# Four modulation rows in one dense product, spread by way of HBM; a tail without identity products; a last block in halves

## The chip, the core and the metric

One core of a Trainium2 chip runs the whole kernel. The metric is the device time of one execution in microseconds (us). The engines are TensorE (PE in the profile, with PEld for its weight loads), VectorE (DVE), ScalarE (ACT), GpSimd (POOL) and SyncE (SP), which here does nothing but issue DMA transfers, in order.

## What is computed

An adaLN block: a modulation from `c`, a sliding-window attention, and an MLP over the tokens. S = 2048 tokens, D = 512, 32 heads of 16, a window of 256, F = 1792.

```python
mod = (silu(c) @ w_mod).reshape(1, 6, 1, 512)          # six rows of 512
sa, ca, ga, sb, cb, gb = mod[:, 0], ..., mod[:, 5]
h = layernorm(x) * (1 + ca) + sa
x = x + ga * (attention(h, wqkv, window=256) @ wo)
h = layernorm(x) * (1 + cb) + sb
u = gelu(einsum('bsd,sf->bdf', layernorm(h), w1) + b1)  # contracts the tokens
y = (u @ w2 + b2).transpose(0, 2, 1)
x = x + gb * y
```

The four rows ga, cb, sb and gb multiply or shift along the free dimension, so the kernel keeps each as a tile of 128 equal rows of 512 (`bc_ga`, `bc_cb1`, which holds 1 + cb, `bc_sb`, `bc_gb`).

## The kernel before

The 2048 tokens are 16 blocks of 128 (`tb`), in four groups of four (`tg`). There are five stages.

- Head (to about 15 us): loads, LayerNorm of group 0, the feature-major rows sa and ca (`modFM`), Q, K and V of the first heads. GpSimd builds constants and masks; a memset of `ones` (L196) releases ScalarE's first copies (L406).
- Attention (about 15 to 171 us): 80 units, 20 for each group. A unit (`ul` = 5 * g8 + k, from 0 to 19) covers eight heads g8 and one of five kinds k of score pieces. For each unit TensorE makes scores into PSUM (`pss`, a ring of three tiles), ScalarE takes their exponential in two instructions (`et`, L573), and TensorE multiplies by V into `po` (L584, L600). After kinds 2 and 4 VectorE transposes `po` (`t`, L632); a reciprocal on VectorE (`zr`), a division on GpSimd (`merge`, L644) and a transpose back on VectorE (`OTd`, L652) follow.
- Tail of the attention (about 171 to 180 us): `t_wo` makes the output projection of the last four blocks: four products with `wod`, then a fifth product that adds the residual through the identity, and a copy out of PSUM by ScalarE (L964 to L969). LayerNorms of these blocks run on VectorE (t1, t2, t3), while TensorE goes on with the first six F-chunks of the MLP (`emit_b1_group0_sc`, L942).
- First MLP product (to 217 us, L942 and L1029), then GELU.
- Second MLP product (to the end, L1049): for each group 14 products per block. The last group runs block after block; VectorE finishes a block in two instructions (L1056, L1061) and SP stores it (L1062).

The order of the attention is written out by hand. `plan(tg)` lays dense work on units (`at[ul]`): Q and K groups, V groups, transposes of the next group's LayerNorm (`transpose_group`), the output projection of the group before (`wo_group`, with LayerNorms 2 and 3 behind it, `ln23`), and in group 0 the four `bc_group`s on units 9, 16, 17 and 18. Each group is 16 matmuls on 32-column strips of the array (`dense`, L274) into the only buffer of the pool `ps_dn`; a group's evacuation by VectorE must be over before the next group starts. In each unit TensorE gets, in this order: the scores of the next unit, the AV product of the unit before if it closes a pair, the dense group, else that AV product.

The steps of VectorE and GpSimd that hang on none of this are chains (`add_chain`), put between the evacuations by a planner: `fill(until)` takes the first chain whose step is ready by the plan's `clock` and fits. `clock` adds up assumed costs; a step that goes on on GpSimd returns its cost there (`on_pool`), and the next step of its chain is not placed before that. Both engines then run their lists strictly in order, so a list that is wrong about a cost makes an engine wait at the head of its queue. `fold_wod` (four multiplications of `wod` by `bc_ga` on GpSimd) is such a chain, added at unit 14 of group 0; `wo_group` needs all four.

Loads are paced: `paced` holds a load back until the first exponential of its unit is over. The parts of `w_mod` for the four rows go out at units 2 to 9 of group 0 (two halves a row, in the order ga, cb, sb, gb), `wo` at units 10 and 11, pieces of `w1` from unit 2 of group 1 on. SP also issues small copies `Vc<-VaugT` (L610).

```python
at.get(ul)                      # one dense group a unit, between scores and AV
for ul, (v, dst, add1) in zip((9, 16, 17, 18), BC):
    lay(ul, bc_group(v, dst, add1, ps_dn))
then[14] = [(lambda g=g: fold_wod(g), 0.0) for g in range(ND)]
```

## Time and profile before

| | us |
|---|---|
| median of 3 runs | 270.45 |
| lowest, highest | 268.9, 270.62 |
| the profiled execution's own time | 271.25 |
| its span, first to last instruction | 269.5 |
| PE busy, DVE busy, ACT busy, POOL busy | 244.3, 165.9, 166.0, 129.0 |
| granted TensorE clock, mean | 0.993 |

A line of the timeline has the start in us, the busy time in us, engine, line of the kernel, operation, output and inputs, shape and count, and in square brackets the idle time before it and what ended that. In a table by windows the columns are window, and for each engine its busy time with the count of instructions, then the granted clock, the DMA engines' busy share and GB/s.

### The profile page before, as it was taken

The page shows a single profiled execution, that of the slowest core. Times are in us where ns is not written, and L with a number is a line of the kernel's source. Part 1 is how long each engine was busy: PE and PEld are TensorE (multiplying, and loading weights), DVE is VectorE, ACT ScalarE, POOL GpSimd, SP SyncE. Part 2 cuts the span into 40 slices and gives each one's busy share as a digit, 9 for nine tenths or more (in the row PEclk, how much of TensorE's full clock was granted, in tenths as well). Part 3 has the DMA queues.
Part 4 walks back from the last instruction along what each step waited for, and adds up shares of the span by engine and source line. Part 5 has one row for each costly group of instructions (what it writes and reads, how often), then busy time and mean ns, then how long its engine had stood idle before and what let it go on. Part 6 is the DMA issues. An engine that isn't in the chain of part 4 may idle for free.

```text
span 269.5 us, 11147 instructions
## 1 busy us (share of the span) xinstructions
PE 244.3 (91%) x4971; PEld 129.4 (48%) x4971; DVE 165.9 (62%) x345; ACT 166.0 (62%) x193; POOL 129.0 (48%) x220
## 2 busy tenths in 40 slices
PE   6978769999899889878889989999999999999993
PEld 2534444455565455545555546544444444444441
DVE  6568965886689787699687886689111000523443
ACT  7777874899999999989999999330091110000000
POOL 6104953876376899888977699864100000000000
PEclk9999997999999999999999999999999999999999
DMA  6918880015654443000122000899900000202021
GB/s 188 356 46 218 243 260 21 5 32 151 182 171 121 130 127 92 6 2 5 31 56 70 5 5 2 272 412 416 394 11 2 0 0 0 80 0 78 27 93 39
DMA packets 25221, 29.31 MB, mean 109 GB/s; under 512 B 3156, under 2 KB 22612, under 8 KB 25172
## 3 DMA queue, kind: packets, MB, share of 16 engines
q1 hardware_dynamic: 25172, 28.59, 33.2%
q8 instruction: 39, 0.64, 1.0%
q14 instruction: 10, 0.08, 0.1%
HBM read 22.03 MB, written 2.10 MB: 90 GB/s over the span
## 4 chain that ended last, share of the span: by engine, by line
PE 66%; DVE 16%; POOL 6%; ACT 5%; issue 3%; DMA 3%; SPq 0%; POOLq 0%; DVEq 0%; ACTq 0%
PE py L1049 18%; PE dn L274 17%; PE pu L942 8%; PE pu L1029 8%; PE pss L523 4%; PE po L584 3%; DVE VaugT L290 3%; PE po L600 3%; DMA wmod<-in_w_mod_dram 3%; DVE t L632 2%; ACT et L573 2%; DVE qs L312 2%; PE pss L530 1%; POOL QT L316 1%; DVE h1T L264 1%
## 5 line engine op out<-in xcount | busy, mean ns | idle before, releaser
L573 ACT ACTIVATE et<-pss 128x1024 bf16<-128x1024 f32 (+1 forms) x160 | 143.7, 992 | 14.0 <-PE pss L530 12.1
L1049 PE MATMUL py<-guT,w2r 128*128 128x512 bf16 x224 | 48.5, 380 | 0.0
L1056 DVE SCALAR_TENSOR_TENSOR o<-py,bFM,bc_gb 128x512 bf16<-128x512 f32 x16 | 11.4, 747 | 44.7 <-PE py L1049 44.7
L274 PE MATMUL dn<-h1T,wqkv 128*32 128x512 bf16 x512 | 34.3, 388 | 3.7 <-DVE qs L312 1.5
L1049 PEld LDWEIGHTS <-w2r 128*128 128x128 bf16 x224 | 21.9, 98 | 26.4
L523 PE MATMUL pss<-QT,KT 32*128 32x64 bf16 (+2 forms) x704 | 28.2, 239 | 5.5 <-ACT et L573 3.0
L632 DVE STREAM_TRANSPOSE t<-po 128x512 f32<-128x512 f32 x32 | 22.6, 706 | 7.8 <-PE po L600 7.7
L214 POOL TENSOR_TENSOR ln_rstd<-ln_ve,mhalf 128x1 f32<-128x1 f32 (+1 forms) x40 | 24.0, 601 | 3.3
L523 PEld LDWEIGHTS <-KT 32*128 32x128 bf16 x704 | 15.0, 93 | 21.2 <-issue 11.8
L584 PE MATMUL po<-et,VaugT 128*32 128x64 bf16 (+2 forms) x704 | 25.2, 242 | 0.0
L210 POOL TENSOR_SCALAR ln_ve<-ln_mv 128x1 f32<-128x1 f32 (+1 forms) x40 | 9.4, 235 | 33.0 <-DVE ln_mv L232 18.4
L584 PEld LDWEIGHTS <-VaugT 128*32 128x32 bf16 x704 | 17.5, 97 | 10.8 <-issue 1.6
L274 PEld LDWEIGHTS <-wqkv 128*32 128x32 bf16 x512 | 13.0, 96 | 13.5 <-issue 6.2
L644 POOL TENSOR_TENSOR merge<-t,zr 128x512 bf16<-128x512 f32 x16 | 16.9, 1056 | 4.8 <-DVE zr L643 4.8
L530 PE MATMUL pss<-mask_q,mask_k 32*128 32x256 bf16 (+1 forms) x256 | 19.1, 264 | 0.0
L274 PE MATMUL dn<-wqkv,h1T 128*32 128x512 bf16 x240 | 15.8, 382 | 1.8 <-DVE VaugT L290 0.8
L676 POOL TENSOR_TENSOR h<-h,bc_cb 128x512 bf16<-128x512 bf16 x12 | 13.9, 1155 | 5.1 <-DVE h L672 5.1
L274 PE MATMUL dn<-wod,OTd 128*32 128x512 bf16 x192 | 12.6, 381 | 3.1 <-DVE KT L309 1.3
L677 POOL TENSOR_TENSOR h<-h,bc_sb 128x512 bf16<-128x512 bf16 x12 | 13.9, 1154 | 0.9
L316 POOL TENSOR_SCALAR QT<-qs,mask_even 128x512 bf16<-128x512 bf16 x14 | 9.7, 692 | 8.8 <-DVE qs L312 8.7
L942 PE MATMUL pu<-hb,w1a 128*128 128x512 bf16 x60 | 13.5, 380 | 0.0
L600 PE MATMUL po<-et,Vc 128*32 128x64 bf16 x960 | 13.1, 195 | 0.0
(113 smaller groups left out, 360.6 us busy)
## 6 DMA issues: line engine op xcount, KB each, us to landing
w2r<-in_B_w_dram SPq DMA_DIRECT2D x14, 512.0 KB, 9.9
w1a<-in_B_w_dram SPq DMA_DIRECT2D x20, 224.0 KB, 3.1
w1b<-in_B_w_dram SPq DMA_DIRECT2D x6, 448.0 KB, 6.9
Vc<-VaugT SPq DMA_DIRECT2D x32, 64.0 KB, 3.0
wmod<-in_w_mod_dram SPq DMA_DIRECT2D x8, 256.0 KB, 5.1
out_dram<-otile SPq DMA_DIRECT2D x16, 128.0 KB, 1.8
x<-in_A_x_dram SPq DMA_DIRECT2D x6, 256.0 KB, 5.1
Vc<-VaugT SPq DMA_DIRECT2D x12, 128.0 KB, 3.3
```

The source lines that it names most:

```text
L214: nc.gpsimd.tensor_tensor(out=r[:], in0=ve[:], in1=mhalf[:, 0:n], op=ALU.pow)
L274: nc.tensor.matmul(out[cols, :], lhsT=lhsT[:, cols], rhs=rhs, start=start, stop=stop, tile_position=(0, 32 * j), skip_group_check=True,)
L523: nc.tensor.matmul(pss[j // 2][:, j % 2, c0 : c0 + nq], lhsT=keys(kb, g8)[rows[j], k0 : k0 + P], rhs=QT[tg][g8][rows[j], par, q0 : q0 + nq ...
L530: nc.tensor.matmul(pss[j // 2][:, j % 2, :].rearrange("p (a r) -> p a r", a=2)[:, 0:n, :] .rearrange("p a (b q) -> p a b q", q=64)[:, :, 0 ...
L573: act = nc.scalar.activation(out=et[:, :, 0:n], in_=state.pop((u, a))[:, :, 0:n], func=ACT.Exp, scale=SCORE_SCALE,)
L584: nc.tensor.matmul(state["po"][32 * j : 32 * j + 32, q0 : q0 + nq], lhsT=VaugT[kb // 4][:, kb % 4, 8 * g8 + 2 * j + par, :], rhs=state["e" ...
L600: nc.tensor.matmul(state["po"][32 * j : 32 * j + 32, q0 : q0 + 64], lhsT=Vc[half][:, b, 8 * g8 + 2 * j + par, :], rhs=state["e", tg, g8, 2 ...
L632: nc.vector.transpose(out=state["t2"][:, par, :], in_=state["po"][:])
L644: nc.gpsimd.tensor_tensor(out=m[:].rearrange("p (b a d) -> p a b d", a=2, d=DH), in0=t2v[:, :, :, 0:DH], in1=zr[:].to_broadcast([P, 2, 16, ...
L942: nc.tensor.matmul(pu[:, i, :], lhsT=w1_of(sc, fc), rhs=hb[sc][:], start=(sc == 0), stop=(sc == NT - 1),)
L1029: nc.tensor.matmul(pu[:, i, :], lhsT=w1_of(sc, fc), rhs=hb[sc][:], start=(sc == s0), stop=(sc == NT - 1),)
L1049: nc.tensor.matmul(pys[tl][:], lhsT=w2r[:, fc, tb * P : (tb + 1) * P], rhs=guT[fc][:], start=(fc == 0), stop=(fc == NF - 1),)
```

## The change

Six edits.

1. `sT_rep` keeps 32 instead of 128 copies of silu(c). One group `bc_group(ps_dn)` on unit 13 makes all four rows at once: strip j of 32 partitions holds row j. One VectorE instruction evacuates it to `mod_rows` and adds `mod_add` (a column that is 1.0 on the second strip). SP writes `mod_rows` to a buffer in HBM and reads it back with four loads of 32 partitions x 4 rows into one tile `bc`. Two memsets on GpSimd make `mod_add`.
2. In group 0, V of the next group moves from units 13 and 19 to units 16 and 18, and the folding of `wod` is added at unit 18 instead of 14.
3. The planner's assumed GpSimd costs change: p2 2.31 to 2.4, p3 1.8 to 2.0, LayerNorm 1's apply 0.95 to 1.13, the allowance after a GpSimd step 0.1 to 0.3.
4. The planner's assumed TensorE times for a unit of kind 2 change: 0.5 to 0.3 and 0.58 to 0.42.
5. `t_wo` drops the product with the identity and ScalarE's copy; VectorE adds the residual while it evacuates.
6. The last block of the last product is made and finished in two halves of 256 columns.

Because the planner reads the changed costs, the lists of VectorE and GpSimd differ in places that the diff does not show. In groups 1 to 3 the scaling `h` (L672) mostly comes later on VectorE, behind the residual additions of `wo_group`; at the end of group 3 two LayerNorm statistics stand between `zr` and the last `OTd`, before it was one; on GpSimd four modulation products stand in a row ahead of the last `merge`, before it was two.

```diff
-    sT_rep = modw.tile([P, ND, P], DT.bfloat16, name="sT_rep")
+    sT_rep = modw.tile([P, ND, 32], DT.bfloat16, name="sT_rep")
+    mod_dram = drampool.tile([P, D], DT.bfloat16, name="mod_dram")
+    nc.gpsimd.memset(mod_add[:], 0.0)
+    nc.gpsimd.memset(mod_add[32:64, :], 1.0)
...
-    def bc_group(v, dst, add1, pool):
+    def bc_group(pool):
         def mms():
             ps_b = pool.tile([P, D], DT.float32, name="dn")
             for k in range(ND):
-                dense(
-                    ps_b, lhsT=sT_rep[:, k, :], rhs=wmod[:, k, v * D : (v + 1) * D],
-                    start=(k == 0), stop=(k == ND - 1),
-                )
+                for j, v in enumerate((2, 4, 3, 5)):
+                    nc.tensor.matmul(
+                        ps_b[32 * j : 32 * j + 32, :], lhsT=sT_rep[:, k, :], rhs=wmod[:, k, v * D : (v + 1) * D],
+                        start=(k == 0), stop=(k == ND - 1), tile_position=(0, 32 * j), skip_group_check=True,
+                    )
         def evac(ps_b):
-            if add1:
-                nc.vector.tensor_scalar_add(out=dst[:], in0=ps_b[:], scalar1=1.0)
-            else:
-                nc.vector.tensor_copy(out=dst[:], in_=ps_b[:])
+            nc.vector.tensor_scalar(
+                out=mod_rows[:], in0=ps_b[:], scalar1=mod_add[:], scalar2=0.0, op0=ALU.add, op1=ALU.add,
+            )
+            dma.dma_start(out=mod_dram[:], in_=mod_rows[:])
+            for j in range(4):
+                dma.dma_start(
+                    out=bc[32 * j : 32 * j + 32, :, :], in_=mod_dram[:].rearrange("(n r) d -> r n d", r=32),
+                )
...
-                return 2.31
+                return 2.4
...
-                return 1.8
+                return 2.0
...
-            return clock["pool"] + 0.1
+            return clock["pool"] + 0.3
...
-                for ul, (v, dst, add1) in zip((9, 16, 17, 18), BC):
-                    lay(ul, bc_group(v, dst, add1, ps_dn))
-                then[14] = [(lambda g=g: fold_wod(g), 0.0) for g in range(ND)]
+                lay(13, bc_group(ps_dn))
+                then[18] = [(lambda g=g: fold_wod(g), 0.0) for g in range(ND)]
...
-                t0, t1, q0, v0, k0, q1, v1 = (10, 11, 12, 13, 14, 15, 19) if tg == 0 else (11, 12, 13, 14, 15, 17, 18)
+                t0, t1, q0, v0, k0, q1, v1 = (10, 11, 12, 16, 14, 15, 18) if tg == 0 else (11, 12, 13, 14, 15, 17, 18)
...
-                    return 0.95
+                    return 1.13
...
-                    first = max(clock["pe"], before) + 0.5
-                    clock["pe"] = max(first, clock["act"] + 0.05) + 0.58
+                    first = max(clock["pe"], before) + 0.3
+                    clock["pe"] = max(first, clock["act"] + 0.05) + 0.42
...
-                    start=(g == 0), stop=False,
-                )
-            nc.tensor.matmul(pa[:], lhsT=identity[:], rhs=xres[tb][:], start=False, stop=True)
-            nc.scalar.activation(out=xres[tb][:], in_=pa[:], func=ACT.Copy)
+                    start=(g == 0), stop=(g == ND - 1),
+                )
+            nc.vector.tensor_tensor(out=xres[tb][:], in0=pa[:], in1=xres[tb][:], op=ALU.add)
...
+            parts = [(4 * tg + tl, 0, D) for tl in range(4)]
+            if tg == NT // 4 - 1:
+                parts[3:] = [(NT - 1, 0, D // 2), (NT - 1, D // 2, D)]
```

## The prediction, as it went on record

> **What bounds the kernel now.** I read the busy shares first, then the 40 slices, then ScalarE's timeline through the attention, TensorE's timeline around its gaps, and the tables by windows. The page says that no engine is the bound throughout.

> ```profile
> PE 244.3 (91%) x4971; PEld 129.4 (48%) x4971; DVE 165.9 (62%) x345; ACT 166.0 (62%) x193; POOL 129.0 (48%) x220
> ACT  7777874899999999989999999330091110000000
> PEclk9999997999999999999999999999999999999999
> ```

> ScalarE stands at 9 from slice 9 (about 57 us) to the end of the attention: groups 1 to 3 go at the pace of the exponentials. Group 0 (slices 2 to 8) does not: 7, 8, 7, 4. There the exponentials wait for scores, and in slice 6 the granted TensorE clock falls. ScalarE's timeline gives the gaps.

> ```profile
> 31.49 2.92 ACT L573 ACTIVATE et<-pss 128x1024 bf16<-128x1024 f32 x4 [1.04 <-PE pss L530]
> 35.99 4.75 ACT L573 ACTIVATE et<-pss 128x1024 bf16<-128x1024 f32 x6 [1.58 <-PE pss L530]
> 43.56 2.92 ACT L573 ACTIVATE et<-pss 128x1024 bf16<-128x1024 f32 x4 [2.82 <-PE pss L530]
> 47.06 4.82 ACT L573 ACTIVATE et<-pss 128x1024 bf16<-128x1024 f32 x6 [0.59 <-PE pss L530]
> 52.85 16.97 ACT L573 ACTIVATE et<-pss 128x1024 bf16<-128x1024 f32 x18 [0.97 <-PE pss L530]
> ...
> 116.88 20.68 ACT L573 ACTIVATE et<-pss 128x1024 bf16<-128x1024 f32 x22 [1.12 <-PE pss L560]
> ```

> Counting two exponentials a unit, the piece at 35.99 begins with unit 11, that at 43.56 with unit 14, that at 52.85 with unit 19. From 52.85 to the end of the attention only 2.4 us of gaps are left (0.17, 0.16, 0.30, 1.12, 0.28, 0.24, 0.16): what group 0 gains, the end gains. What makes the gaps is on TensorE.

> ```profile
> 34.73 0.61 PE L274 MATMUL dn<-wmod,sT_rep 128*32 128x512 bf16 x8 [1.28 <-DMA wmod<-in_w_mod_dram]
> ...
> 38.44 0.62 PE L256 MATMUL dn<-identity,xn 128*128 128x128 bf16 x8 [0.74 <-DVE h1T L264]
> ...
> 40.15 1.84 PE L274 MATMUL dn<-h1T,wqkv 128*32 128x512 bf16 x16 [0.59 <-DVE h1T L264]
> ...
> 51.04 1.05 PE L274 MATMUL dn<-wmod,sT_rep 128*32 128x512 bf16 x16 [0.41 <-DVE bc_cb L334]
> ```

> At unit 9 the group for ga waits 1.28 us for its weights, and the scores of unit 11 stand behind it. Then two transposes, each evacuated by VectorE into `h1T`, and the Q group follow one another through the one buffer. The Q group at 40.15 takes 1.84 us where the same 16 products take 1.05 at 51.04: the clock.

> ```profile
> 39.00:40.00 1.00, 0.56 (x14) 0.21 (x12) 0.90 (x2) 1.00 (x2) 0.78 (x1) 1.00 0.79 258
> ...
> 41.00:42.00 1.00, 1.00 (x20) 0.43 (x16) 0.00 (x0) 0.00 (x0) 0.00 (x0) 0.50 0.10 32
> ```

> The column before the last two is the granted clock: 1.00, then 0.50 from about 40.4 to 43.7. TensorE was busy 0.70, 0.56 and 0.56 of the three microseconds before.

> **The change part by part.** All terms go against the profiled execution: span 269.5, own time 271.25, 0.80 above the median of the runs.

> *Head.* Two memsets on GpSimd stand ahead of `ones`, which releases ScalarE's first copies at 3.40, on the chain that ended last. The smallest memsets of the trace take 0.09 to 0.10 us: +0.2 (0 if the chain has other slack, 0.25 at most).

> *Unit 9 without a group.* The scores of unit 11 no longer stand behind the wait. The transposes of unit 10 then need `xn`, whose last tile GpSimd ends at 34.47 + 0.76 = 35.23. So they start at 35.25, not 36.34. VectorE lacks `bc_ga` (0.69) ahead of the first `h1T`, and its statistics run before. So `h1T` starts when the transposes end (35.87), at about 35.95 and not at 37.43; the second transposes at 36.95 (38.44), the Q group at 38.65 (40.15): -1.5. Bounds: 0, if GpSimd's `xn` slips as well, and -2.0, the whole of VectorE's wait for `bc_ga`.

> *The clock.* From 40.15 to the first exponential of unit 14 pass 3.41 us, nearly all of it at the half rate. At full rate the Q group takes 1.05 (-0.79), and the 1.2 us of AV products and scores up to 43.17 about half: together -1.4. Without the stall TensorE is busy, by the times above, for 0.62 + 0.80 + 0.62 + 0.30 + 0.40 = 2.7 of the 3.4 us before the Q group, or 0.8, against 0.6 before. The windows 16 to 27 and 27 to 37 had 9.97 of 11.00 and 7.46 of 10.00 at clock 1.00. So I take the dip as gone: -1.4 (bounds 0 and -1.6, half of the 3.3 us). [...]

> *Unit 13.* The one group is the same 16 products (1.05) and takes the place of a V group; the one evacuation has the size of `bc_cb` (0.69). It needs all eight pieces of the weights. The last is issued at 35.73 and these land in 4.5 to 5.3 us, by 41.0, when the queue goes empty (DMA share 0.10). TensorE comes to it at about 40.9, and the last piece is used in the second half: a wait of 0 to 0.3, hidden by 0.5 us between the next scores and their exponential: 0.

> *Way by HBM.* Evacuated at about 42.7, the rows are written (the stores of 128 KB land in 1.8, a loaded queue took 6.8), then SP issues four loads of about 0.5 each, and the last lands about 3 later (copies of 64 and 128 KB: 3.0 and 3.3): about 7.5 us, at 50.2. Behind it on SP stand only the `Vc` copies, issued at 56.54 before. On GpSimd the first fold comes to the head at about 49.4 and waits up to 0.8. With the third fold behind a `merge` and `xn` between, the last fold ends at about 60.3; the first `wo` product, 68.18 before, comes at about 64. That cover of 3.7 us costs it at 0.

> *Units 16 to 19.* Unit 16 keeps a group (V), 17 and 19 lose theirs. The scores of unit 19 stood behind the group at 51.04, and that is the gap of 0.97: -0.97 (bounds -0.5, if VectorE's `qs` holds them, and -1.0). The gap of 0.59 at 47.06 stands. VectorE loses 3 x 0.69 and most of 1.13 (`sT_rep`), hidden by the exponentials: 0.

> *The lists of groups 1 to 3.* The 1.12 at 116.88 comes from VectorE: `h` (L672) at its head waited 1.34 us for GpSimd's `ln_rstd`, and the residual addition behind it was late. The new list puts the additions first; against that `h`, and the GpSimd products after it, come later everywhere. Bounds: -1.1 and +1.5 (a new gap like that in one or two of three groups). I take 0, the middle of ends equally far.

> *Tail.* Four identity products at the pace of this stage (224 products in 48.5 us, 0.216 each): -0.86. But the last `OTd`, at 173.61 before, comes after one more statistic (0.68 + 0.18): `zr` ends at 172.44, two statistics end at about 174.1, so it runs 0.45 later, and TensorE's fourth product waits for it: +0.45. The four additions on VectorE (0.69 each, where ScalarE took 0.60) delay the last `hb` from 190.2 to about 192.4; TensorE wants it from 195.1 - 0.86 + 0.45 = 194.7: hidden by 2.3 us. Sum -0.4 (bounds -0.9 and +1).

> *Last block.* Products of 256 columns on the full array are not in the trace; ones of 128 columns follow one another at 57 ns ((0.62 - 0.22) / 7), of 512 at 216: by the line between, 110 ns, so 28 x 0.110 - 14 x 0.216 = +0.06. After the last product, 0.75 + 0.43 on 512 columns; operations on four columns take 0.15, so half takes about 0.45 and 0.29: -0.44. The store of half the size: -0.1 (64 against 128 KB differ by 0.3 above). Sum -0.47 (bounds -0.2 and -0.9).

> Sum: +0.2 - 1.5 - 1.4 - 0.97 + 0 - 0.4 - 0.47 = -4.54 us. On 271.25 that is 266.7, and on the median of the runs 265.9.

> **The rivals.**

> *The dip of the clock stays.* For it: the chain of two transposes and two evacuations is the same, and its waits of 0.74 and 0.59 remain; and the three runs before lie 1.6 us apart (268.9 against 270.45 and 270.62), as if some had it and some not. Against it: the busier window. It gives -4.54 + 1.4 = -3.14: 267.3.

> *The lists give back what group 0 gains.* GpSimd is busy 9.09 and 9.14 of 10.00 us in 87 to 97 and 97 to 107; if its order decides there, the scaling that now comes later makes it late for the transposes, with gaps like 1.12 in two groups and the last `merge` 0.6 late: +2.8, which leaves -1.7: 268.7. Against it: GpSimd stood idle 4.53 us at 74.59.

> *Slower: the way by HBM is late and GpSimd stands at the first fold.* Behind it in its queue wait the last `merge` of group 0, `xn` and the masked Q; the first `wo` product cannot start before the fourth fold. The cover is 3.7 us, so it costs from a way of 11.2 us on, and makes the kernel slower from 15.7 us on: two landings of 6.8 like the slowest of `wmod`, with 2.0 us of issue between, give 15.6. Against it: those were in a full queue (share 0.8 to 0.95), and here the share is 0.00 to 0.03. A write of 6.8 and then four loads one after another at 3.0 make 18.8, 7.6 past the cover: 273.5.

> *More than forecast.* The gap at 116.88 goes and nothing comes in its place: -5.6, 264.8.

> **How the numbers follow.** A measurement of this kernel can tell about 1%, 2.7 us, from no change. Chances: forecast 0.42, dip stays 0.27, lists give back 0.20, more than forecast 0.06, slower 0.05. The time is that of the likeliest, 265.9. Range: from 264.2 (the larger gain with 0.6 of the tail's and last block's lower bounds) to 268.9 (the lists' case with 0.2 to spare). Faster by over 1% means under 267.75: 0.42 + 0.27 + 0.06 = 0.75. Within 1%: 0.20. Slower by over 1%: 0.05.

> **What would show it.** In ScalarE's timeline no gap of 1.58 ahead of unit 11, one of about 1 us ahead of unit 14, none ahead of unit 19; clock 1.00 throughout group 0; no wait for `wmod` at the new group; the first fold waiting under 1 us on the loads of `bc`; the attention ending about 3.7 us earlier; 0.4 us less from there to the end of the first MLP sums; the last product followed by about 0.75 us of VectorE. Wrong it would be if GpSimd becomes the releaser of `h1T` or `OTd` in groups 1 to 3, if the dip moves rather than goes, or if TensorE waits for `hb` in the tail.

## The result, and the profile after

The changed kernel took 266.66 us (median of 11 runs, 265.74 to 269.11) beside 268.9 us before (11 runs, 268.35 to 270.62): ratio 0.9907, 95% interval 0.9879 to 0.9936. Measured again later beside other runs of before it came to 0.9878 (0.9844 to 0.9912). So it is faster by 0.9 to 1.2%, some 2.5 to 3.3 us. Ratios leave out runs that took over 1.5% longer than the fastest of the same kernel. The profiled run of the changed kernel took 268.42 us with a span of 266.7; before, that was 271.25 and 269.5.

From the page of the changed kernel, busy times, ScalarE and the granted clock by slices:

```profile
PE 243.6 (91%) x4933; PEld 129.7 (49%) x4933; DVE 166.9 (63%) x348; ACT 163.7 (61%) x189; POOL 129.4 (49%) x222
...
ACT  6748887999999999999999999300091110000000
...
PEclk9799979999999999999999999999999999999999
```

The clock did not become steady: it now has two dips, in slices 1 and 5. ScalarE's timeline of the changed kernel in group 0:

```profile
33.83 4.93 ACT L584 ACTIVATE et<-pss 128x1024 bf16<-128x1024 f32 x6 [1.04 <-PE pss L541]
39.31 2.92 ACT L584 ACTIVATE et<-pss 128x1024 bf16<-128x1024 f32 x4 [0.55 <-PE pss L571]
43.58 2.92 ACT L584 ACTIVATE et<-pss 128x1024 bf16<-128x1024 f32 x4 [1.35 <-PE po L611]
46.91 22.12 ACT L584 ACTIVATE et<-pss 128x1024 bf16<-128x1024 f32 x24 [0.42 <-PE pss L541]
```

Counted as in the prediction, the pieces begin with units 9, 12, 14 and 16. The gap of 1.58 ahead of unit 11 is gone, one of 0.55 has come ahead of unit 12, that ahead of unit 14 went from 2.82 to 1.35, and that ahead of unit 19 (0.97) is gone: from 46.91 the exponentials run for 22.12 us without one. All exponentials together waited 10.0 us, 14.0 before. TensorE around unit 13 of the changed kernel:

```profile
37.26 1.00 PE L261 MATMUL dn<-identity,xn 128*128 128x128 bf16 x8
...
39.35 1.03 PE L261 MATMUL dn<-identity,xn 128*128 128x128 bf16 x8
...
41.48 1.05 PE L279 MATMUL dn<-h1T,wqkv 128*32 128x512 bf16 x16 [0.46 <-DVE h1T L269]
...
43.32 1.05 PE L333 MATMUL dn<-wmod,sT_rep 128*32 128x512 bf16 x16
```

The one group at 43.32 waits for nothing. The Q group at 41.48 takes 1.05, so the dip is no longer there; but the transposes ahead of it take 1.00 and 1.03, against 0.62 before: the dip has come earlier. By windows (columns as before), chosen at the edges of the dips:

```profile
6.61:10.02 3.41, 2.64 (x54) 1.92 (x53) 2.02 (x10) 3.39 (x7) 1.02 (x2) 1.00 1.14 351
10.02:13.43 3.41, 3.41 (x26) 1.22 (x26) 1.08 (x4) 1.71 (x5) 0.00 (x0) 0.50 1.07 367
33.92:37.33 3.41, 2.26 (x83) 1.42 (x68) 2.49 (x7) 3.34 (x5) 3.20 (x6) 1.00 0.74 207
37.33:40.74 3.41, 3.41 (x64) 2.23 (x68) 2.28 (x5) 2.86 (x4) 2.10 (x4) 0.50 0.88 277
```

Both dips last 3.41 us and start 27.31 us apart, which is 8.0 times 3.41.

The way by HBM, on GpSimd and in the list of transfers of the changed kernel:

```profile
52.05 0.70 POOL L219 TENSOR_TENSOR ln_rstd<-ln_ve,mhalf 128x2 f32<-128x2 f32 x1
52.72 2.27 POOL L789 TENSOR_TENSOR wod<-wod,bc 128x512 bf16<-128x512 bf16 x2
57.02 1.06 POOL L655 TENSOR_TENSOR merge<-t,zr 128x512 bf16<-128x512 f32 x1 [2.02 <-DVE zr L654]
58.03 1.16 POOL L789 TENSOR_TENSOR wod<-wod,bc 128x512 bf16<-128x512 bf16 x1
...
62.73 1.16 POOL L789 TENSOR_TENSOR wod<-wod,bc 128x512 bf16<-128x512 bf16 x1
```

```profile
bc<-mod_dram SPq DMA_DIRECT2D x4, 128.0 KB, 3.4
```

The first two folds follow `ln_rstd` with no bracket, so they did not wait for `bc`. The write goes out at 45.2 and the last load at 49.3; by the median of 3.4 from issue to landing it lands at about 52.7: 7.5 us from the evacuation, as estimated. In `after_2`, below, the first fold follows `ln_rstd` in the same way. The last fold ends at 63.89, the first `wo` product starts at 67.39.

The stages, from the timelines (head: to the first exponential; attention: to the end of the last one; end: from the last product to the end of the span):

| us | before | changed |
|---|---|---|
| head | 15.13 | 17.48 |
| attention | 155.45 | 151.43 |
| tail and first MLP product | 46.38 | 45.74 |
| second MLP product | 48.51 | 48.55 |
| end | 4.07 | 3.46 |

The head is longer by 2.35 us mostly by its dip, which lies on the idle products and the first 32 strips of V. This is one run: in the second profile of the changed kernel, `after_2` below, the head has no dip and takes 15.70.

### The profile page after: what moved, and what is told of

It is laid out like the page before. It is cut to its first block, busy times and chain, and to the rows that moved or that the text cites. A ratio compares the mean times of both kernels' runs of the same rounds, so it can differ in the third digit from the quotient of the medians.

```text
span 266.7 us, 11081 instructions
## 1 busy us (share of the span) xinstructions
PE 243.6 (91%) x4933; PEld 129.7 (49%) x4933; DVE 166.9 (63%) x348; ACT 163.7 (61%) x189; POOL 129.4 (49%) x222
## 4 chain that ended last, share of the span: by engine, by line
PE 70%; DVE 18%; ACT 5%; issue 3%; DMA 2%; SPq 1%; ACTq 0%; DVEq 0%
PE py L1073 18%; PE dn L279 18%; PE pu L1037 8%; PE pu L951 7%; PE pss L534 5%; ACT et L584 5%; PE po L595 4%; DVE t L643 3%; PE po L611 3%; DVE qs L317 2%; DVE VaugT L295 2%; DMA wmod<-in_w_mod_dram 2%; PE pss L541 2%; DVE KT L314 2%; DVE x L378 1%
## 5 line engine op out<-in xcount | busy, mean ns | idle before, releaser
L1073 PE MATMUL py<-guT,w2r 128*128 128x512 bf16 (+1 forms) x238 | 48.5, 366 | 0.0
L1052 DVE SCALAR_TENSOR_TENSOR o<-py,bFM,bc 128x512 bf16<-128x512 f32 (+1 forms) x17 | 11.7, 715 | 44.4 <-PE py L1073 44.4
L534 PE MATMUL pss<-QT,KT 32*128 32x64 bf16 (+2 forms) x704 | 29.6, 237 | 7.6 <-ACT et L584 4.7
L1073 PEld LDWEIGHTS <-w2r 128*128 128x128 bf16 x238 | 23.3, 98 | 25.3
L215 POOL TENSOR_SCALAR ln_ve<-ln_mv 128x1 f32<-128x1 f32 (+1 forms) x40 | 9.5, 237 | 37.2 <-DVE ln_mv L237 20.4
L534 PEld LDWEIGHTS <-KT 32*128 32x128 bf16 x704 | 15.7, 92 | 23.8 <-issue 14.0
L279 PE MATMUL dn<-wqkv,h1T 128*32 128x512 bf16 x240 | 15.7, 380 | 1.3 <-DVE qs L317 0.8
L687 POOL TENSOR_TENSOR h<-h,bc 128x512 bf16<-128x512 bf16 x12 | 14.0, 1169 | 3.9 <-DVE h L683 3.9
L688 POOL TENSOR_TENSOR h<-h,bc 128x512 bf16<-128x512 bf16 x12 | 13.9, 1156 | 0.9
```

What stands on the lines that cost most here:

```text
L279: nc.tensor.matmul(out[cols, :], lhsT=lhsT[:, cols], rhs=rhs, start=start, stop=stop, tile_position=(0, 32 * j), skip_group_check=True,)
L534: nc.tensor.matmul(pss[j // 2][:, j % 2, c0 : c0 + nq], lhsT=keys(kb, g8)[rows[j], k0 : k0 + P], rhs=QT[tg][g8][rows[j], par, q0 : q0 + nq ...
L1073: nc.tensor.matmul(pys[n][:, 0 : hi - lo], lhsT=w2r[:, fc, tb * P : (tb + 1) * P], rhs=guT[fc][:, lo:hi], start=(fc == 0), stop=(fc == NF ...
```

## The experiments

Theory P, the prediction's: the stall ahead of unit 11 and the dip behind it belong to the kernel before; filling the stall takes the dip away. Against it theory L: the dips are luck of the run. (The expectation of `rows_alone` has letters of its own: what it calls theory A is L, and its rival B is that the memsets lengthen the head by 2.3 us in every run.) When the first four experiments had spoken against P and given L no support, a third was formed: theory W, below.

### One part at a time

Four kernels, each the kernel before with one part of the change.

`rows_alone`: the one dense group at unit 13, the way by HBM, the two memsets, units and folds as in the change; the planner's costs as before.

> The kernel before with the four rows in one group, the way by HBM and the moved V groups and folds, and nothing else of the change. Theory A (the dip of the clock in group 0 is luck of the run: the runs of before mostly have none, so the 1.4 us of the clock term belong to no edit): 1.0 to 1.6 us faster than before, and the runs of both kernels fall into levels about 1.5 to 2.4 us apart that go with the mean granted clock (0.993 for one dip, 0.986 for two). Rival B (the change removes 4 us from the attention in every run and the two memsets on GpSimd lengthen the head by 2.3 us in every run): 1.3 to 1.9 us faster, and the first exponential starts at 17 us or later in this kernel and at 15.1 us in kernels without the memsets.

`tail_alone`:

```
-                    start=(g == 0), stop=False,
+                    start=(g == 0), stop=(g == ND - 1),
-            nc.tensor.matmul(pa[:], lhsT=identity[:], rhs=xres[tb][:], start=False, stop=True)
-            nc.scalar.activation(out=xres[tb][:], in_=pa[:], func=ACT.Copy)
+            nc.vector.tensor_tensor(out=xres[tb][:], in0=pa[:], in1=xres[tb][:], op=ALU.add)
```

> The kernel before with the tail without identity products alone. Only one statistic stands between zr and the last OTd here, as before, so the late OTd (+0.45 us) should be absent: 0.86 us faster. If TensorE waits for the last hb, or if the two buffers of the tail are freed too late by VectorE: 0 to 0.4 us faster, with a wait for hb or pa on TensorE.

`half_alone`: `finish` and `parts` of the change, nothing else.

> The kernel before with the last block in halves alone: 0.47 us faster, in the end after the last product. Rival: the store of half the size lands no sooner and the 14 further weight loads cost, 0.2 us or less.

`lists_alone`: the planner's costs alone.

```
-                return 2.31
+                return 2.4
...
-                return 1.8
+                return 2.0
...
-            return clock["pool"] + 0.1
+            return clock["pool"] + 0.3
...
-                    return 0.95
+                    return 1.13
...
-                    first = max(clock["pe"], before) + 0.5
-                    clock["pe"] = max(first, clock["act"] + 0.05) + 0.58
+                    first = max(clock["pe"], before) + 0.3
+                    clock["pe"] = max(first, clock["act"] + 0.05) + 0.42
```

> The kernel before with the changed costs of the planner alone. From the three other parts (1.1, 0.9, 0.5 us) and the whole (2.24 us) 0 to +0.5 us is left for the lists, most of it a late last OTd. If the lists remove the gap of 1.12 us in group 2 and cost nothing elsewhere: 1.1 us faster. If GpSimd decides the order in groups 1 to 3: 1.5 us or more slower.

Measured, with the stages of each profiled run. A dip of 3.41 us takes the mean clock of a run of 267 us to 0.994, so the mean clock of each timed run tells whether it had one; the last column counts runs under 0.9955.

| | median us | ratio (95%) | attention | tail, first MLP | end | runs with a dip |
|---|---|---|---|---|---|---|
| rows_alone | 268.63 | 0.9984 (0.9952 to 1.0015) | 153.10 | 46.38 | 3.96 | 7 of 12 |
| tail_alone | 268.10 | 0.9959 (0.9932 to 0.9987) | 153.53 | 45.52 | 4.07 | 0 of 12 |
| half_alone | 269.19 | 1.0002 (0.9969 to 1.0034) | 154.45 | 46.38 | 3.45 | 4 of 12 |
| lists_alone | 268.30 | 0.9975 (0.9947 to 1.0002) | 151.79 | 46.61 | 4.06 | 1 of 12 |
| before, beside them | 269.02 | | | | | 6 of 35 |

The attention of `tail_alone` is that of the kernel before. ScalarE's timeline in its profiled run:

```profile
31.77 7.79 ACT L573 ACTIVATE et<-pss 128x1024 bf16<-128x1024 f32 x10 [1.04 <-PE pss L530]
41.07 2.92 ACT L573 ACTIVATE et<-pss 128x1024 bf16<-128x1024 f32 x4 [1.51 <-PE po L600]
44.35 4.82 ACT L573 ACTIVATE et<-pss 128x1024 bf16<-128x1024 f32 x6 [0.36 <-PE pss L530]
50.13 16.97 ACT L573 ACTIVATE et<-pss 128x1024 bf16<-128x1024 f32 x18 [0.96 <-PE pss L530]
```

No gap ahead of unit 11, 1.51 and not 2.82 ahead of unit 14, the same 0.96 ahead of unit 19: without the change. `lists_alone`, with the same group for ga at unit 9, has neither the stall nor the dip either. `half_alone`, which is the kernel before up to its last block, has both: TensorE waits for the weights of ga at unit 9, and the clock halves from 36.71.

```profile
36.73 1.05 PE L274 MATMUL dn<-wmod,sT_rep 128*32 128x512 bf16 x8 [0.95 <-DMA wmod<-in_w_mod_dram]
```

So in the four profiles with a group for ga at unit 9 the stall and the dip come together, twice, or not at all, twice: that much of theory P holds. But the stall (weights that landed late) belongs to some runs and not to the kernel. Of 82 runs of the kernel before beside all these experiments, 15 had a dip; they were 1.9 to 2.7 us longer than the others measured with them. And filling the stall does not take the dip away: with the one group and nothing at unit 9 to wait for, `rows_alone` had a dip in 7 of 12 runs. Theory P falls by that; theory L, luck alone, has no reason why 6 of 35 should become 7 of 12. The five runs of `rows_alone` with a clock of 0.997 or more (267.74 to 268.24, mean 267.96) are 0.9 under the mean of before without a dip (268.87), close to the gap of unit 19 (0.97); the dips took most of it back. The rival B of `rows_alone` falls with the heads of five later profiles: with the memsets and without a dip there, the first exponential starts at 15.42 to 15.96 and not at 17 or later.

The tail's 0.86 came out whole in `tail_alone`, and the last block's end is shorter by 0.62 in `half_alone`, less than its timing can tell. Of the lists, the gaps of the exponentials in groups 1 to 3 tell more than one profile's stage: with the old costs they add up to 2.43 (before), 3.48, 2.63 and 3.42 (`tail_alone`, `half_alone`, `rows_alone`), mean 2.99; with the new ones to 2.27 (`lists_alone`), 1.96 and 1.50 (the changed kernel's two profiles) and 1.50, 1.77 and 2.30 in `after_fill9`, `after_thin9` and `after_fill9_warm` below, mean 1.88. So they bring 1.1 us by the profiles, where the timing of `lists_alone` says 0.7 (0 to 1.4). One gap carries most of it: the 1.12 at 116.88 (unit 52) stands in all four profiles with the old costs (1.12 to 1.16) and in none of the ten with the new ones.

### What makes a dip

`after_fill9`: the changed kernel with a group that nobody reads at unit 9.

```
+            if (tg, ul) == (0, 9):
+                pd = ps_dn.tile([P, D], DT.float32, name="dn")
+                for dc in range(ND):
+                    dense(pd, lhsT=wqkv[:, dc, 0:P], rhs=h1T[0][:, dc, :], start=(dc == 0), stop=(dc == ND - 1))
             group = at.get(ul)
```

> The changed kernel with 16 strips of 32 columns (four times a dense product over four column tiles, read by nobody) put back at unit 9 of group 0, where the change left TensorE without a group; the lists are the same. Theory W (work): the granted clock halves for one window of 3.41 us when the window before held less than about 0.37 of what the full array can multiply (worked out from the traces so far: 0.35, 0.34, 0.30, 0.22, 0.30, 0.36, 0.30 ahead of the seven dips, 0.39 and more ahead of the windows without one); the 16 strips are four full products of 0.216 us, 0.25 of a window, so the windows of 33 to 38 us rise from 0.28 to 0.53 and the dip of the attention is gone: at most 2 of the runs with a mean clock between 0.990 and 0.995, where the changed kernel has 6 of 11. Theory L (luck of the run alone): as often as without the strips. Time: 1.05 us more of TensorE, of which 0.56 falls into waits for the exponentials: 266.0 to 266.9 where the clock is full, ratio 0.989 to 0.993.

`after_thin9`: there, five products that use 32 by 32 of the array each; `after_thin16`: sixteen of them.

```
+                pd = ps_dn.tile([P, D], DT.float32, name="dn")
+                for n in range(5):
+                    nc.tensor.matmul(pd[0:32, :], lhsT=wqkv[0:32, 0, 0:32], rhs=h1T[0][0:32, 0, :], start=True, stop=True)
```

> The same place, but five products of 32 rows by 32 columns of the array, 512 columns each (some 1.1 us of TensorE, 0.005 of a window's work). Theory W: the work stays at 0.28 to 0.30, the dips stay as frequent as in the changed kernel (at least 5 of 11 runs with a mean clock under 0.995), and the time is the changed kernel's or up to 0.7 more: 266.6 to 267.4. Theory O (occupation: a window counts as idle by the time in which TensorE runs nothing): the busy share of the windows at 33 to 38 us rises from 0.67 to 0.9 as in the run with 16 strips, and the dips go as they go there.

> As after_thin9, with 16 products of 32 rows by 32 columns in place of five: some 3.5 us in which TensorE is never idle and does 0.02 of a full array's work. Theory W: whatever the phase of the windows, one of them holds less than 0.37, so a dip in group 0 in every run (no run with a mean clock over 0.996) and a time of 3 to 5 us over after_2 (3.5 us of products less 0.56 of waits that they fill, and what the dip costs). Theory O (a window counts by the time in which TensorE runs nothing): TensorE is busy for over 0.9 of these windows, no dip in group 0 in any run, and 2 to 3 us over after_2.

`after_2`: the changed kernel again.

> The changed kernel once more, unchanged, beside the next three on the same chip. Theory W (work in windows of 3.41 us) and theory L alike: about 0.99 of the time before; a mean clock under 0.995 in more than half of its runs; in its profile every dip of the clock follows a window with less than 0.37 of the full array's work and no window with 0.39 or more is followed by one.

| | median us (lowest, highest) | ratio (95%) | runs with a dip |
|---|---|---|---|
| changed kernel, first | 266.66 (265.74, 269.11) | 0.9907 (0.9879 to 0.9936) | 10 of 11 |
| after_2 | 266.22 (265.10, 267.14) | 0.9878 (0.9844 to 0.9912) | 4 of 6 |
| after_fill9 | 265.60 (265.45, 266.46) | 0.9878 (0.9830 to 0.9927) | 0 of 6 |
| after_thin9 | 265.54 (265.43, 266.55) | 0.9883 (0.9829 to 0.9936) | 2 of 6 |
| after_thin16 | 271.47 (268.57, 273.54) | 1.0035 (0.9998 to 1.0073) | 10 of 10 |

The kernels were timed in three sets, beside medians of before of 268.90 (the first row), 269.38 (`after_2`, `after_thin16`) and 268.40 (`after_fill9`, `after_thin9`); across sets compare the ratios. Against its forecast `after_fill9` came out 0.4 us fast, `after_thin9` 1.1, and `after_thin16` lies 5.25 over `after_2` where 3 to 5 were expected.

The two expectations on thin products give their work too low: one uses 32 by 32 of 128 by 128, a 16th of a full product, so five are 0.02 of a window and sixteen do 0.06 of a full array's work while they run. `after_thin9` has a dip in 2 of 6 runs; so few runs tell neither theory from the other. The sixteen do. The windows of `after_thin16` ahead of and in its dip, and then two windows of `after_fill9`, of which the first covers unit 9:

```profile
33.57:36.98 3.41, 2.82 (x46) 1.34 (x43) 2.70 (x7) 2.92 (x4) 3.20 (x7) 1.00 0.80 246
36.98:40.39 3.41, 3.41 (x12) 0.98 (x10) 0.00 (x0) 0.00 (x0) 1.23 (x3) 0.50 0.91 284
40.39:43.80 3.41, 3.41 (x104) 2.57 (x100) 1.36 (x3) 1.94 (x2) 0.00 (x0) 0.50 0.20 65
```

```profile
32.12:35.53 3.41, 2.82 (x97) 1.64 (x97) 2.75 (x7) 3.10 (x5) 3.20 (x7) 1.00 0.71 203
35.53:38.94 3.41, 2.66 (x100) 1.72 (x89) 2.60 (x6) 3.41 (x4) 2.34 (x4) 1.00 0.97 290
```

TensorE is busy for the same 2.82 us in the first window of each. The one with 0.13 of a full array's work was followed by a clock of 0.50, the one with 0.55 by 1.00. The thin products fill the window from 36.98 without a pause, and the clock stays at half for another window. Theory O falls, and L with it: dips in all ten runs of one kernel and in none of six of another.

Over all 14 profiles of before, the changed kernel and the experiments there are 1063 whole windows. At full clock 22 held 0.384 or less and every one was followed by a dip (in the head, the attention and the run-out behind the last product); 1026 held 0.391 or more and none was. The other 15 were at half clock: 13 of them held 0.34 to 0.50 and full clock followed, two held 0.05 (`after_thin16`, from 36.98) and 0.31 (`after_spread_warm`, from 38.46) and a second window at half clock followed, so that those two dips lasted 6.83 us. So among these 15, too, the work parts the two kinds, somewhere between 0.31 and 0.34. Other counts do not part the windows at full clock: by busy time, 2.82 us was followed by a dip (33.57) and 1.43 was not (265.41); with the rows of the array alone counted, 0.76 was (changed, 33.92) and 0.56 was not (before, 6.12); with its columns alone, 0.88 was (before, 36.84) and 0.57 was not (changed, 13.44); with the work less the transposes, 0.38 was (`after_thin16`, 265.67, which holds none) and 0.30 was not (before, 6.12). Windows of both sides, among them the nearest to the boundary on each, with the time that TensorE was busy:

| window (us) | kernel | busy us | work | next |
|---|---|---|---|---|
| 33.57 | after_thin16 | 2.82 | 0.13 | dip |
| 33.92 | changed | 2.26 | 0.30 | dip |
| 6.61 | changed | 2.64 | 0.35 | dip |
| 36.84 | before | 2.08 | 0.36 | dip |
| 265.67 | after_thin16 | 1.41 | 0.38 | dip |
| 265.41 | half_alone | 1.43 | 0.39 | none |
| 36.29 | after_fill9_warm | 2.37 | 0.44 | none |
| 33.43 | before | 2.13 | 0.48 | none |
| 32.12 | after_fill9 | 2.82 | 0.55 | none |

The kernel before shows the prediction's error best. The wait for the weights (to 34.73) lies in the first of these windows, which held 0.48; the dip came behind the second, which held 0.36, though TensorE was busy for nearly as long (2.08 us, 2.13 in the first):

```profile
33.43:36.84 3.41, 2.13 (x76) 1.45 (x71) 1.41 (x4) 1.82 (x3) 2.62 (x5) 1.00 0.82 224
36.84:40.25 3.41, 2.08 (x67) 1.26 (x68) 2.95 (x8) 3.41 (x6) 1.05 (x1) 1.00 0.87 288
40.25:43.66 3.41, 3.41 (x72) 1.76 (x72) 1.15 (x2) 0.59 (x3) 0.84 (x2) 0.50 0.17 59
```

Why the stall and the dip still went together there: I slid a window of 3.41 us over 22 to 42 us of each trace, in steps of 0.05, and looked for the least work. Without the stall the kernel before never falls under 0.41 (`tail_alone`, `lists_alone`), so by the counts above no phase of the windows gives a dip; with it the least is 0.23 (before) and 0.26 (`half_alone`). The changed kernel has no stall and falls to 0.29 and 0.24 (`after_2`) all the same, by the missing group; with the filling group the least is 0.44. `after_thin9` falls to 0.25, so by the same counts its profile without a dip is luck of the phase.

### Can the dips be had away for less?

`after_spread`: the changed kernel's own groups laid so that no two units next to each other are empty. `after_spread_warm`: the same, and `warm(4)` (four idle products) between the two halves of the head. `after_fill9_warm`: `after_fill9` with those.

```
-                for ul, g8, kind in ((2, 1, "q"), (3, 1, "k"), (4, 2, "q"), (5, 2, "k"), (6, 3, "q"), (7, 3, "k")):
+                for ul, g8, kind in ((2, 1, "q"), (3, 1, "k"), (4, 2, "q"), (5, 2, "k"), (7, 3, "q"), (9, 3, "k")):
-                lay(8, bias_group(ps_dn))
+                lay(6, bias_group(ps_dn))
```

> The changed kernel with its own groups spread otherwise: the transposition of the biases at unit 6 in place of 8, Q of heads 24 to 31 at 7 in place of 6, K of the same at 9 in place of 7; units 6 and 8 hold next to nothing, and nothing is added. Theory W: no window of 3.41 us at 28 to 38 us with less than 0.40 of work, so no dip there (at most 2 of the runs with a mean clock between 0.990 and 0.995) and no product more: 265.9 to 266.4, ratio 0.987 to 0.991. Theory L: as the changed kernel, 266.6, with as many dips. A third outcome: the transposes of unit 10 come to wait for the evacuation of K (0.69 us) and the exponential gaps of group 0 grow by up to 0.7: 267.0.

> As after_spread, and four more products of the idle kind (128 by 512, 0.216 us each at full clock) in the head, behind the transposes of the first two tiles, where TensorE waits for the second piece of the modulation weights (0.28 to 0.67 us). Theory W: the window at 6 to 10 us rises by up to 0.25, from 0.20 to 0.36 in the runs that had a dip in the head, so that no run stays under 0.990; time 265.9 to 266.6 in every run, a spread of less than 1 us where the changed kernel has 265.7 to 269.1. If the four products stand ahead of the sums with the second piece (it lands early in some runs) they cost up to 0.6 us. Theory L: runs under 0.990 as before, some 4 of 11.

> after_fill9 and the four idle products in the head. Theory W: neither in the head nor in group 0 a window under 0.37, so no run with a mean clock under 0.996; against after_2 it gains what its dips cost, 0 to 2 us a run: ratio to before 0.984 to 0.990, median 0.5 to 1.5 us under after_2's. If the four products stand in the way where the second piece of weights lands early, up to 0.6 is lost again and it ties with after_2.

`after_spread` took 268.02 us (ratio 0.9969, 0.9937 to 1.0001) and had dips in 12 of 12 runs, `after_spread_warm` 268.32 (0.9975, 0.9941 to 1.0009) in 10 of 12: theory W's times were wrong here, because a wait came that I had looked for elsewhere. TensorE in `after_spread`:

```profile
36.64 0.45 PE L261 MATMUL dn<-identity,xn 128*128 128x128 bf16 x5 [1.87 <-POOL xn L226]
```

GpSimd masks Q of heads 24 to 31 at the same time as before (16.4 us behind the first exponential, as in `after_2`), but `ln_ve` and `ln_rstd` of another LayerNorm now stand ahead of the last `xn` in its list. That `xn` starts 20.4 us behind the first exponential, 19.2 in `after_2`, and the transposes of unit 10 wait 1.87 us; that stall makes a window of 0.33 (35.36 to 38.77) and the dip. By theory W that is what had to follow; the placement was a bad one. `after_fill9_warm` had no dip in 7 runs, as expected (266.14 us, 265.87 to 268.42, ratio 0.9897, 0.9861 to 0.9932), but no gain: the head is some 0.5 longer with the four products (first exponential at 16.13, and at 16.20 in `after_spread_warm`, against 15.42 to 15.96, mean 15.68, in the five profiles that have the memsets but neither the four products nor a dip in the head). So none of these versions beats the changed kernel by more than can be measured: the filling group takes the dips away and costs about what they cost.

### How long may the way by HBM be?

`after_hops`: three copies within HBM put between the write and the loads.

```
+    mod_hops = [drampool.tile([P, D], DT.bfloat16, name=f"mod_hop{n}") for n in range(3)]
...
-            dma.dma_start(out=mod_dram[:], in_=mod_rows[:])
+            dma.dma_start(out=mod_hops[0][:], in_=mod_rows[:])
+            dma.dma_start(out=mod_hops[1][:], in_=mod_hops[0][:])
+            dma.dma_start(out=mod_hops[2][:], in_=mod_hops[1][:])
+            dma.dma_start(out=mod_dram[:], in_=mod_hops[2][:])
```

> The changed kernel with three more copies in HBM between the write of the four rows and the four loads, each behind the last: the way gets some 9 us longer (three landings of 2 to 3 us and their issue). By the prediction (the way is hidden up to 3.7 us beyond its own length, then every microsecond counts) it costs about 5.3 us: 272. By the trace of the changed kernel GpSimd has 2.0 us of idle time among the folds and 3.5 us lie between the last fold and the first wo product, so 5.5 are hidden and it costs 2 to 5, about 3.5: 270. If the loads are hidden anyway: 266.7, and no wait of the fold for a DMA over 1 us on the way to the wo products.

270.44 us (269.35 to 274.04), ratio 1.0056 (1.0026 to 1.0086): 4.2 over `after_2`, nearest to the 270 that was expected from the changed kernel's trace. The folds start 7.0 us later than there, counted from the first exponential (58.20 - 15.85 against 51.08 - 15.70). The three waits that tell how it comes to the end, on GpSimd, VectorE and TensorE of `after_hops`:

```profile
58.20 2.26 POOL L793 TENSOR_TENSOR wod<-wod,bc 128x512 bf16<-128x512 bf16 x2 [7.77 <-DMA bc<-mod_dram]
```

```profile
61.51 0.71 DVE L667 STREAM_TRANSPOSE OTd<-merge 128x512 bf16<-128x512 bf16 x1 [4.27 <-POOL merge L659]
62.15 0.65 DVE L315 CAST KT<-dn 128x512 bf16<-128x512 f32 x1
```

```profile
62.85 1.10 PE L280 MATMUL dn<-h1T,wqkv 128*32 128x512 bf16 x16 [3.25 <-DVE KT L315]
```

GpSimd stands at the fold; `merge` behind it is late; VectorE stands at the transpose of `merge`; the evacuation of K behind that is late; TensorE's next group waits for the only buffer. 3.25 of waiting and a dip behind it (the window from 60.30 held 0.22) make the 4.2. It comes by the K group at 62.85 and not by the `wo` products, which the prediction had priced; those are late by 4.0 only with everything else. Counted from the first exponential the K group starts 2.9 later than in `after_2` (62.85 - 15.85 against 59.84 - 15.70), so of the 7.0 some 4.1 are hidden; the dip behind it costs another 1.1, which leaves about 3. The prediction said 3.7.

## Why the prediction came out, by its steps

The time was forecast as 265.9 and came as 266.66 and 266.22, yet the forecast gain was 4.54 us, 2.5 to 3.3 were measured, and the two largest terms were wrong. All terms were held against the one profiled run (271.25), though the text itself saw the three runs before lie 1.6 us apart, "as if some had it and some not"; the median of the kernel before is 268.4 to 269.4 in four other sets of runs. A base some 1.5 us too high and 2.9 us of gains that were not there for most runs made up much of each other: that the time came so near is luck.

- *Head*, +0.2: mis-sized, about +0.4. Without a dip in the head the first exponential starts at 15.13, 15.41 and 15.27 without the memsets and at 15.42 to 15.96 (mean 15.68 of five) with them; that it is the memsets is not shown.
- *Unit 9 without a group*, -1.5: wrong for most runs. The step that failed is the reading of the 1.28 us wait as the kernel's; `tail_alone` and `lists_alone` have it not, `half_alone` has 0.95.
- *The clock*, "I take the dip as gone", -1.4: wrong. The step that failed: TensorE's busy time, 0.8 against 0.6, taken as what tells whether a dip comes. The window ahead of the changed kernel's dip was busy for 2.26 of 3.41 us, 0.66, and not 0.8; but in the 14 profiles the dips went with the work (0.384 or less ahead of each, 0.30 ahead of the changed kernel's at 37.33), and the change took work out: dips in 14 of the changed kernel's 17 runs, 15 of 82 before. What one costs was 1.9 to 2.7 before (with the late weights, as far as two profiles tell) and about 1.3 in `after_2` (265.10 and 265.21 without one, 266.21 to 267.14 with one). Averaged over the runs that is some 0.4 before and 1.1 after: a loss of 0.6. The rival that the dip stays came nearer to the measured gain (its -3.14) than the forecast; the dip moved to the transposes, which the prediction had named as a sign that it was wrong.
- *Unit 13*, 0: right; no wait in the profile, 0.21 for `wmod` in `after_fill9`.
- *The way by HBM*, 0, 7.5 us long: right in both; the cover is 4.1 up to the K group and 3 with the dip behind it, near the 3.7, but it ends elsewhere.
- *Units 16 to 19*, -0.97: right; the gap of unit 19 is gone in every profile with the one group.
- *The lists*, 0: mis-sized, -1.1 by the profiles, which was the bound that I had; the middle between ends was no estimate.
- *Tail*, -0.86 + 0.45: -0.64. The late `OTd` costs 0.22 more than in `tail_alone` (45.74 against 45.52; `lists_alone` has +0.23 beside before), half of what was taken; TensorE never waits for `hb`.
- *Last block*, -0.47: -0.57 (-0.61 at the end, +0.04 in the products); the halves take 0.48 and 0.29, 0.45 and 0.29 were taken:

```profile
263.24 0.48 DVE L1052 SCALAR_TENSOR_TENSOR o<-py,bFM,bc 128x256 bf16<-128x256 f32 x1 [0.72 <-PE py L1073]
263.75 0.29 DVE L1057 TENSOR_TENSOR otile<-o,x 128x256 bf16<-128x256 bf16 x1
```

The sum with what was measured: +0.4 (head) + 0.6 (clock and unit 9) - 0.97 - 1.1 - 0.64 - 0.57 = -2.3 us, beside -2.5 (-1.7 to -3.3) and -3.3 (-2.4 to -4.2) timed. The parts timed alone add up to -0.8%, some 2.2 us. What stays open is what one dip costs in the changed kernel: the first set of runs has only one without a dip, at 266.33, no faster than those with one.

## What to carry to other kernels

Before a gap or a dip is priced, look whether the kernel's other runs have it: the mean clock of each run told here, without a trace, that the dip was in about one run of six. Before dense work is taken off TensorE in a stretch where the array is mostly fed by small tiles, count what work is left there: here, with 0.30 left in a window of 3.41 us, the clock fell to 0.50 behind it, though TensorE was busy for 2.26 us of it. And when engines run their lists in order, follow a late transfer through every list that it stands in: here the evacuation of K two engines on decided (TensorE stood 3.25 us for it), not the product that used the data.

## What the runs showed of the hardware

- In the 14 profiles, by the counts above: of 1048 windows of 3.41 us at full clock the 22 with 0.384 or less of the full array's work were followed by a granted clock of 0.50, the 1026 with 0.391 or more by 1.00. Of 15 windows at half clock the 13 with 0.34 or more were followed by full clock, and the two with 0.05 (`after_thin16`, from 36.98) and 0.31 (`after_spread_warm`, from 38.46) by another at half, though TensorE was busy for all of the first.
- The dips of one run begin whole numbers of 3.41 us apart (10.02 and 37.33 in the changed kernel, 9.67 and 36.98 in `after_thin16`: 27.31, 8 times 3.41). Where the windows lie differs from run to run: dips in the head began at 9.41 (`half_alone`), 10.02 (changed), 10.74 (`rows_alone`) and 9.67 us (`after_thin16`).
- The idle products at the start (128 by 128, 512 columns) follow one another at 0.43 us up to the first record of the clock (6.1 to 6.9 us in before, the changed kernel and `tail_alone`), and right behind it, in before, at 0.216. The clock column says 1.00 throughout, yet 0.43 is also their pace in the dip of the changed kernel (from 10.23, clock 0.50): ahead of its first record the column does not show their pace.
